# A bound on |h| from column norms and token norms, with squares on GpSimd, in place of a maximum over every block

## The chip, the cores and the metric

The kernel runs on one core of one Trainium2 chip. The metric is the device time of one execution in microseconds (us); here 1173.38 us is the median of three runs before the change (1172.96 to 1173.91). The engines are named as in the profile: PE (TensorE matmuls), PEld (its weight loads), DVE (VectorE), ACT (ScalarE), POOL (GpSimd) and SP (SyncE, which here only issues DMAs). A letter q behind an engine's name (SPq, PEldq) means its queue: instructions that the sequencer handles by itself.

## The reference

Attention with a sigmoid in place of the softmax, and a two-layer block on its result:

```python
# q, k, v: (8, 12, 448, 64)   w_in: (768, 2048)   w_out: (2048, 768)
scores = scale * np.matmul(q, k.transpose(0, 1, 3, 2)) - np.log(S)
attn = 1.0 / (1.0 + np.exp(-scores))
x = np.matmul(attn, v)          # (8, 12, 448, 64), laid out as 3584 tokens x 768
h = x @ w_in
g = h - np.tanh(h)
out = g @ w_out
```

q and k are scaled so that scores have a spread of some units, and the two weight matrices arrive as 64-bit floats.

## The kernel before

The eight batches are handled one after the other. Batch 0 is computed with 32-bit matmuls; from batch 1 on, every matrix is split into a high and a low 16-bit half and each product is three 16-bit matmuls. `first` runs batch 0 and all work on the weights, in an order that is written out by hand as a string (`ORDER`, one letter for each step). `batch` runs one later batch: `moe1` (h and g, from the lines of `product` and `mix`) and `moe2` (g times w_out), with the attention of the next batch put between the matmuls of `moe2`. PE, ACT, DVE and POOL execute what they get in exactly this written order; nothing reorders it.

**The weights' way in.** w_in comes in 24 pieces of 128 x 512 64-bit values. `convert` sends each through stages, one stage a step (letter r): `conv_load` (DMA), `conv_sign` (ACT, L180), `conv_bits` (three DVE instructions: L190 shifts, L191 and L196 each combine two tiles of SBUF), and `conv_end`. The result of L191, the tile `sta`, is |w| as a 32-bit float. `conv_end` takes its high 16 bits and has PE add up the columns: with the matrix `rows` for two pieces at a time (L221, into `cs`); when a group of six pieces is through, ACT squares the sums (L227). `w_in_scales` then turns the four rows of squares into one number by a matmul (L284, `cn`), a maximum, a transpose (L289, `pt`), a maximum and another matmul (L294, `pb`): `W2`, a bound for every column's squared length. All PE instructions for pieces 0 to 21 stand ahead of the first matmul of h (letter M, L1006).

**The small case.** The code holds two versions of the program: class `Small` has a short polynomial for g that is good for |h| below 1/4, and `Builder` has a longer one for all h. `Small` always runs. It keeps, of every block of h squared (`u`), the maximum (L1161, `squares`), and after the last block `largest` turns these 64 columns into one number, `flag`, by a DVE maximum (L1171), a PE transpose (L1173) and a DVE maximum (L1174). `build_kernel` then has all five engines load `flag` into a register (L1183) and compare it (L1186). Where it is above `SMALL_BITS` the whole of `Builder` runs again; else the code jumps past it to the waits for the last DMAs and the end of the program.

Of the kernel before, what the change touches and what calls it, by code (L numbers as in the profile page):

```python
# [9 lines left out]
BF16 = mybir.dt.bfloat16  # L10
F32 = mybir.dt.float32
# [3 lines left out]
AF = mybir.ActivationFunctionType  # L15
ALU = mybir.AluOpType
AX = mybir.AxisListType
# [7 lines left out]
CUT = 0.65  # L25


SMALL_BITS = 0x3D7FFFFF
KAPPA_S = 0.051974997
B_S, C_S = -1.2822222, 4.7692432  # L30

# [7 lines left out]
class Builder:  # L39
# [190 lines left out]
    def convert(self, pieces, when):  # L230

        ps = [{"piece": q, "k": k, "when": when} for k, q in enumerate(pieces)]
        wait, end = [None, None], [None, self.conv_end]
        if when == "mixture":
            wait, end = [None] * 3, [None] + end
        elif when == "product":
            wait, end = [None], [None, None] + end
        stages = [self.conv_load] + wait + [self.conv_sign, self.conv_bits] + end
        for t in range(len(ps) + len(stages) - 1):
            for k in range(len(stages) - 1, -1, -1):  # L240
                if stages[k] and 0 <= t - k < len(ps):
                    stages[k](ps[t - k])
            yield 1
# [33 lines left out]
    def w_in_scales(self):  # L277


        nc = self.nc  # L280
        n = self.DFF // 4
        cn = self.ps.tile([P, 512], F32, name="cn", tag="av", bufs=1)
        for j, sq in enumerate(self.row):
            nc.tensor.matmul(cn[32 * j : 32 * (j + 1), :n], self.onesb[:, :32], sq, start=True, stop=True)  # L284
        st = self.sm.tile([P, 1], F32, name="st", tag="st")
        nc.vector.tensor_reduce(st, cn[:, :n], axis=AX.X, op=ALU.max)
        yield 0
        pt = self.ps.tile([P, 512], F32, name="pt", tag="tr", bufs=1)
        nc.tensor.transpose(pt[:1, :P], st, self.ident)  # L289
        mx = self.sm.tile([1, 1], F32, name="mx2", tag="mx2")  # L290
        nc.vector.tensor_reduce(mx, pt[:1, :P], axis=AX.X, op=ALU.max)
        yield 0
        pb = self.ps.tile([P, 512], F32, name="pb", tag="tr", bufs=1)
        nc.tensor.matmul(pb[:, :1], self.onesf[:1, :], mx, start=True, stop=True)  # L294
        self.W2 = self.const.tile([P, 1], F32, name="W2")
        nc.vector.tensor_scalar(self.W2, pb[:, 0:1], 1.03, None, op0=ALU.mult)
        self.Swi, self.iSwi = self.scale_of(self.W2, "swi")
# [462 lines left out]
    def g_scales(self, m):  # L760

        t1 = lambda name: self.sm.tile([P, 1], F32, name=name)
        V = self.nc.vector
        hb = t1("hb")
        V.tensor_scalar(hb, m, self.W2, None, op0=ALU.mult)
        hc = t1("hc")
        V.tensor_scalar(hc, hb, 1e12, None, op0=ALU.min)
        h2 = t1("h2")
        V.tensor_tensor(h2, hc, hc, op=ALU.mult)
        h3 = t1("h3")  # L770
        V.scalar_tensor_tensor(h3, h2, 1.0 / 9.0, hc, op0=ALU.mult, op1=ALU.mult)
        g2 = t1("g2")
        V.tensor_tensor(g2, hb, h3, op=ALU.min)
        V.tensor_scalar(g2, g2, 2.1, TINY, op0=ALU.mult, op1=ALU.max)
        y = self.pow2(g2, 1, "g")
        iSg = t1("iSg")
        V.tensor_scalar(iSg, y, 2.0**49, None, op0=ALU.mult)
        Sg = t1("Sg")
        V.reciprocal(Sg, iSg)
        return Sg, iSg  # L780


    def halves(self, m, g):

# [322 lines left out]
    def second(self, b, blocks, alone, events):  # L1107

        step = lambda: next(self.blocks)
        events += [(p, step) for p in blocks]  # L1110
        scales = []

        def norms():
            scales.append(self.batch_scales(self.xs, False))
            next(scales[0])

        if blocks:
            end = blocks[alone]
            events.append((end + 3, norms))
            events += [(p, lambda: next(scales[0], None)) for p in (end + 5, end + 7)]  # L1120
        events.sort(key=lambda e: e[0])
        full = self.NF * (self.S // P)
        for k, _ in enumerate(self.moe2(b, self.gs)):
            now = k + 1 if k < full else full + (k + 1 - full) / 2
            while events and events[0][0] <= now:
                events.pop(0)[1]()
        assert not events


class Small(Builder):  # L1130
# [4 lines left out]
    def __init__(self, ctx, tc, flag, *args):  # L1135
        super().__init__(ctx, tc, *args)
        V = self.nc.vector
        self.flag = flag
        self.squares = self.const.tile([P, self.B * self.NB], F32, name="squares")
        V.memset(self.squares, 0.0)  # L1140
        self.bs = self.const.tile([P, 1], F32, name="bs")
        V.memset(self.bs, B_S)
        self.seen = 0

    def mix(self, ps, g, ih, ihk):

        nc = self.nc
        V = nc.vector
        temp = lambda name: self.tp.tile([P, 2, self.S], F32, name=name, tag="t")
        u = temp("u")  # L1150
        n, self.seen = self.seen, self.seen + 1
        nc.scalar.activation(u, ps, AF.Square, scale=ih)  # L1152
        m = temp("m")
        V.scalar_tensor_tensor(m, ps, ihk, u, op0=ALU.mult, op1=ALU.mult)  # L1154
        yield 1
        self.finish_g()
        yield 1
        q = temp("q")
        nc.scalar.activation(q, u, AF.Square, bias=self.bs)  # L1159
        V.scalar_tensor_tensor(m, q, C_S, m, op0=ALU.add, op1=ALU.mult)  # L1160
        V.tensor_reduce(self.squares[:, n : n + 1], u, axis=AX.XY, op=ALU.max)  # L1161
        if self.seen == self.B * self.NB:
            self.largest()
        yield 1
        self.late.append((m, g))

    def largest(self):

        nc = self.nc
        m = self.sm.tile([P, 1], F32, name="largest")  # L1170
        nc.vector.tensor_reduce(m, self.squares, axis=AX.X, op=ALU.max)  # L1171
        pt = self.ps.tile([P, 512], F32, name="lt", tag="tr", bufs=1)
        nc.tensor.transpose(pt[:1, :P], m, self.ident)  # L1173
        nc.vector.tensor_reduce(self.flag, pt[:1, :P], axis=AX.X, op=ALU.max)  # L1174


def build_kernel(tc, *args):
    nc = tc.nc
    with tc.tile_pool(name="flag", bufs=1) as pool:
        flag = pool.tile([1, 1], F32, name="flag")  # L1180
        with ExitStack() as ctx:
            Small(ctx, tc, flag, *args).build()
        bits = nc.values_load(  # L1183
            flag.bitcast(mybir.dt.int32), skip_runtime_bounds_check_because="it is compared, nothing else"
        )
        with tc.If(bits > SMALL_BITS):  # L1186
            with ExitStack() as ctx:
                Builder(ctx, tc, *args).build()

# [28 lines left out]
```

## Time and profile before

| | |
|---|---|
| three runs, median (lowest, highest) | 1173.38 us (1172.96, 1173.91) |
| the profiled execution's own time | 1173.52 us |
| its span, first to last instruction | 1171.5 us |
| mean granted TensorE clock | 0.997 |
| PE busy | 1154.7 us (99%) |
| DVE busy | 761.6 us (65%) |
| ACT busy | 678.0 us (58%) |
| POOL busy | 77.8 us (7%) |

The page gives each engine's busy time in total and in 40 slices of the span; groups of equal instructions by line with their mean duration and what ended the idle time ahead of them; the chain of work that ended last, followed back from the end; and the timeline, which has each instruction's start and duration. The device time is the span and 2.0 us around it.

### The profile page before, as it was taken

How to read it: one execution, taken by the hardware profiler on the slowest of the kernel's cores; microseconds unless marked ns; L12 is line 12 of the kernel's file. 1: busy time of each engine (PE TensorE's matmuls, PEld its weight loads, DVE VectorE, ACT ScalarE, POOL GpSimd, SP SyncE). 2: the span in 40 equal slices, each digit the busy share in tenths (PEclk: the TensorE clock that was granted, in tenths of full speed). 3: DMA queues.
4: the chain of work that ended last, by engine and by line, in shares of the span. 5: the costliest groups of instructions: out<-in, count | busy, mean ns of one | idle time of the engine just before them, and what ended most of it. 6: DMA issues, size and time to landing. Idle time of an engine off the chain costs nothing.

```text
span 1171.5 us, 18358 instructions
## 1 busy us (share of the span) xinstructions
PE 1154.7 (99%) x7586; PEld 601.8 (51%) x7586; DVE 761.6 (65%) x1170; ACT 678.0 (58%) x993; POOL 77.8 (7%) x58
## 2 busy tenths in 40 slices
PE   9999999999999999999999999999999999999897
PEld 3355444555555555555555555555555555555464
DVE  6988698766767656776577666676566755645600
ACT  7975785545884457844686348753578446623300
POOL 0000010000220002100020002200031000200000
PEclk9999999999999999999999999999999999999999
DMA  9942251000321002210021001210022100000001
GB/s 364 355 157 69 80 182 54 28 1 10 92 69 53 1 16 75 62 39 1 30 77 56 29 1 55 84 53 1 16 62 62 53 1 30 15 21 1 1 15 37
DMA packets 34059, 70.47 MB, mean 60 GB/s; under 512 B 3888, under 2 KB 21040, under 8 KB 33968
## 3 DMA queue, kind: packets, MB, share of 16 engines
q1 hardware_dynamic: 33744, 68.89, 18.0%
q8 instruction: 61, 1.00, 0.4%
q10 hardware_dynamic: 224, 0.33, 0.1%
q14 instruction: 30, 0.25, 0.1%
HBM read 58.20 MB, written 11.01 MB: 59 GB/s over the span
## 4 chain that ended last, share of the span: by engine, by line
PE 92%; DVE 3%; DMA 3%; ACT 1%; issue 0%; SPq 0%; DVEq 0%; ACTq 0%
PE ph L794 33%; PE po L880 30%; PE acc L441 8%; PE sc L410 8%; PE ph L1006 6%; PE por L928 5%; DMA raw<-moe_w_in 1%; DVE wo L257 1%; DMA vn<-v 1%; DMA wo<-moe_w_in 1%; PE wl L211 0%; DVE wo L256 0%; PE nm L711 0%; PE pbn L360 0%; DVE stb L190 0%
## 5 line engine op out<-in xcount | busy, mean ns | idle before, releaser
L880 PE MATMUL po<-wo,g 128*128 128x384 f16 x2304 | 390.4, 327 | 1.4 <-DVE g L788 0.7
L794 PE MATMUL ph<-xhl,wi 128*128 128x448 f16 x2016 | 382.6, 352 | 0.0
L880 PEld LDWEIGHTS <-g 128*128 128x128 f16 x2304 | 221.2, 98 | 167.5 <-issue 25.7
L794 PEld LDWEIGHTS <-wi 128*128 128x128 f16 x2016 | 196.7, 98 | 185.0 <-issue 2.1
L428 DVE SCALAR_TENSOR_TENSOR ahl<-a,ahl 128x896 f16<-128x896 f32 x126 | 161.6, 1318 | 140.4 <-ACT ahl L427 140.4
L1152 ACT ACTIVATE u<-ph,ih 128x896 f32<-128x896 f32 x64 | 64.4, 1006 | 248.3 <-PE ph L794 230.6
L421 ACT ACTIVATE a<-sc,nls,rn 128x896 f32<-128x896 f32 x147 | 156.1, 1092 | 57.1 <-PE sc L410 55.6
L1154 DVE SCALAR_TENSOR_TENSOR m<-ph,ihk,u 128x896 f32<-128x896 f32 x64 | 73.6, 1150 | 150.2 <-ACT u L1152 150.1
L427 ACT ACTIVATE ahl<-a 128x896 f16<-128x896 f32 x126 | 113.1, 940 | 0.6
L410 PE MATMUL sc<-Q,K 64*128 64x448 f16 x1008 | 100.6, 353 | 0.7 <-ACT a L421 0.7
L441 PE MATMUL acc<-ahl,vhl 128*64 128x448 f16 (+1 forms) x864 | 80.6, 356 | 0.0
L472 POOL TENSOR_TENSOR x<-x 128x448 f32<-128x448 f32 x24 | 27.1, 1130 | 763.7 <-ACT x L455 763.7
L1006 PE MATMUL ph<-x,wi 128*128 128x448 f32 x192 | 74.1, 540 | 0.0
L788 DVE SCALAR_TENSOR_TENSOR g<-m,Sg,g 128x896 f16<-128x896 f32 x64 | 73.2, 1143 | 0.8
L787 ACT ACTIVATE g<-m,Sg 128x896 f16<-128x896 f32 x64 | 66.1, 1034 | 12.7 <-DVE m L1160 10.8
L1160 DVE SCALAR_TENSOR_TENSOR m<-q,m 128x896 f32<-128x896 f32 x64 | 69.4, 1084 | 0.9
L1161 DVE TENSOR_REDUCE squares<-u 128x1 f32<-128x896 f32 x64 | 69.0, 1078 | 0.0
L1159 ACT ACTIVATE q<-u,bs 128x896 f32<-128x896 f32 x64 | 66.0, 1031 | 0.3
L928 PE MATMUL por<-wo,g 128*64 128x384 f16 x768 | 64.9, 327 | 0.0
L410 PEld LDWEIGHTS <-K 64*128 64x128 f16 x1008 | 35.5, 97 | 52.4 <-issue 30.9
L441 PEld LDWEIGHTS <-vhl 128*64 128x64 f16 (+1 forms) x864 | 38.3, 108 | 40.2 <-issue 19.8
L928 PEld LDWEIGHTS <-g 128*64 128x64 f16 x768 | 42.4, 110 | 22.1 <-issue 4.5
(143 smaller groups left out, 842.6 us busy)
## 6 DMA issues: line engine op xcount, KB each, us to landing
knn<-k SPq DMA_DIRECT2D x45, 224.0 KB, 2.6
qnn<-q SPq DMA_DIRECT2D x44, 224.0 KB, 2.6
rawo<-moe_w_out SPq DMA_DIRECT2D x22, 384.0 KB, 5.2
out<-o SPq DMA_DIRECT2D x21, 384.0 KB, 2.3
raw<-moe_w_in SPq DMA_DIRECT2D x13, 512.0 KB, 8.2
vn<-v SPq DMA_DIRECT2D x24, 256.0 KB, 2.9
wo<-moe_w_in SPq DMA_DIRECT2D x11, 512.0 KB, 8.1
vn<-v SPq DMA_DIRECT2D x24, 192.0 KB, 2.4
```

The lines of the kernel that those rows point to most:

```text
L410: self.nc.tensor.matmul(ps[i * m : (i + 1) * m, h, : self.S], K[i][r, w, c * P : c * P + m], Q[i][r, x, :], start=(n == 0), stop=(n == len ...
L421: self.nc.scalar.activation(a[:, 0], ps[:, :, : self.S], AF.Sigmoid, bias=self.nls, scale=scale)
L427: nc.scalar.activation(A[:, 0], a[:, 0], AF.Copy, scale=A_SCALE)
L428: nc.vector.scalar_tensor_tensor(A[:, 1], a[:, 0], A_SCALE, A[:, 0], op0=ALU.mult, op1=ALU.subtract)
L441: self.nc.tensor.matmul(acc[i][h * D : (h + 1) * D, : self.S], v[k, w, 2 * QT + h if half else h * QT + c], A[k, x, h], start=(n == 0 and ...
L788: nc.vector.scalar_tensor_tensor(g[:, 1], m, Sg, g[:, 0], op0=ALU.mult, op1=ALU.subtract)
L794: self.nc.tensor.matmul(ph, self.wi[:, self.slot(c, k), part, e * P : (e + 1) * P], xhl[c][:, x, :], start=(i == 0), stop=(i == len(prods) ...
L880: nc.tensor.matmul(po[i][:, :H], gs[f // 2][:, x, f % 2, tk * P : (tk + 1) * P], self.wo[:, i * self.NF + 2 * ks[f // 2] + f % 2, w], star ...
L928: nc.tensor.matmul(po[e * D : (e + 1) * D, :H], gs[f // 2][:, x, f % 2, nm:S], self.wo[:, e * self.NF + 2 * ks[f // 2] + f % 2, w], start= ...
L1006: nc.tensor.matmul(ph[:, e, :S], self.fp32(self.wi, self.slot(c, k))[:, 0, e * P : (e + 1) * P], xs[c], start=(c == 0), stop=(c == self.NC ...
L1154: V.scalar_tensor_tensor(m, ps, ihk, u, op0=ALU.mult, op1=ALU.mult)
L1160: V.scalar_tensor_tensor(m, q, C_S, m, op0=ALU.add, op1=ALU.mult)
```

## The change

Three parts.

- `Small.convert` replaces the sum of |w| by exact squares. A new stage, `conv_square`, stands in the step that was empty between `conv_bits` and `conv_end`: POOL multiplies the high 16 bits of `sta` with themselves into a 16-bit tile `sq` (24 times, 128 x 512). `conv_end` has PE add these up with a matrix of ones, one matmul for each piece over all 128 columns; after six pieces DVE takes the maximum of the sums (`tops`). `w_in_scales` is one maximum over the four columns of `tops`; the matmuls into `cn` and `pb` and the transpose `pt` are gone.
- The maximum over `u` in `mix` and `largest` are gone. `g_scales`, which had the product of `W2` and the largest squared token length for its own use (`hb`, a bound on h squared), now also keeps the maximum of these products in `flag`. `SMALL_BITS` is lowered from 0.0625 to 0.0615. ACT writes the square of u + b back into `u` instead of into a new tile.
- `flag` is loaded into the registers 20 steps into the last `moe2`, by an event, and the branch has its small case placed first behind the compare.

```diff
     def g_scales(self, m):
         V.tensor_scalar(hb, m, self.W2, None, op0=ALU.mult)
+        self.g_bounds(hb)
...
     def second(self, b, blocks, alone, events):
+        if b + 1 == self.B:
+            events.append((20, self.decide))
...
 class Small(Builder):
-        self.squares = self.const.tile([P, self.B * self.NB], F32, name="squares")
-        V.memset(self.squares, 0.0)
+        V.memset(flag, 0.0)
+        self.tops = self.const.tile([P, 4], F32, name="tops")
+    def convert(self, pieces, when):
+        if when != "attention":
+            yield from super().convert(pieces, when)
+            return
+        ps = [{"piece": q, "k": k, "when": when} for k, q in enumerate(pieces)]
+        stages = [self.conv_load, None, None, self.conv_sign, self.conv_bits, self.conv_square, self.conv_end]
...
+    def conv_square(self, p):
+        n = p["piece"][3]
+        high = p["a"].bitcast(BF16).rearrange("p (n t) -> p n t", t=2)[:, :, 1]
+        p["sq"] = self.sm.tile([P, n], BF16, name="sq", tag="sq", bufs=4)
+        self.nc.gpsimd.tensor_tensor(p["sq"], high, high, op=ALU.mult)
+    def conv_end(self, p):
...
+        self.nc.tensor.matmul(self.cs[:, :n], self.onesb, p["sq"], start=(r == 0), stop=(r == self.NC - 1))
+        if r == self.NC - 1:
+            self.nc.vector.tensor_reduce(self.tops[:, i : i + 1], self.cs[:, :n], axis=AX.X, op=ALU.max)
+    def w_in_scales(self):
+        m = self.sm.tile([P, 1], F32, name="mx2", tag="mx2")
+        self.nc.vector.tensor_reduce(m, self.tops, axis=AX.X, op=ALU.max)
...
+    def g_bounds(self, hb):
+        self.nc.vector.tensor_tensor(self.flag, self.flag, hb, op=ALU.max)
     def mix(self, ps, g, ih, ihk):
-        q = temp("q")
-        nc.scalar.activation(q, u, AF.Square, bias=self.bs)
-        V.scalar_tensor_tensor(m, q, C_S, m, op0=ALU.add, op1=ALU.mult)
-        V.tensor_reduce(self.squares[:, n : n + 1], u, axis=AX.XY, op=ALU.max)
-        if self.seen == self.B * self.NB:
-            self.largest()
+        nc.scalar.activation(u, u, AF.Square, bias=self.bs)
+        V.scalar_tensor_tensor(m, u, C_S, m, op0=ALU.add, op1=ALU.mult)
...
+    def decide(self):
+        self.bits = self.nc.values_load(
...
-        with tc.If(bits > SMALL_BITS):
+        with tc.If(fast.bits > SMALL_BITS, preferred_fallthrough_block=False):
```

How this moves instructions is seen at three places. The first is POOL at the start of the program, during the way in of w_in; `ident` is a constant, `x_...` are tiles of squared attention results. Before:

```order
masks.py:197 MEMSET ident 128x128
masks.py:199 ISA
masks.py:199 AFFINE_SELECT ident<-ident 128x128 [waits Pool_49]
L481 TENSOR_TENSOR x_1158<-x_1158,x_1295 128x448 [waits DVE_49,PE_49,Activation_49]
L481 TENSOR_TENSOR x_1158<-x_1158,x_1443 128x448 [waits Activation_49]
```

And after:

```order
masks.py:197 MEMSET ident 128x128
masks.py:199 ISA
masks.py:199 AFFINE_SELECT ident<-ident 128x128 [waits Pool_49]
L1170 TENSOR_TENSOR sq<-sta 128x512 [waits DVE_49] x4
L1170 TENSOR_TENSOR sq<-sta 128x512 [waits DVE_49,PE_49] x20
L481 TENSOR_TENSOR x_1176<-x_1176,x_1313 128x448 [waits DVE_49,PE_49,Activation_49]
```

POOL had nothing to do there; now 24 squares stand in its queue, each behind a DVE instruction (L191), and from the fifth on also behind the matmul that reads the buffer. The same stretch on DVE, around the end of the first group of six pieces, before:

```order
L190 TENSOR_SCALAR sta<-sta 128x512
L191 SCALAR_TENSOR_TENSOR sta<-raw,sta 128x512
L196 SCALAR_TENSOR_TENSOR wi<-raw,sta 128x2x256
L190 TENSOR_SCALAR sta<-sta 128x512
L191 SCALAR_TENSOR_TENSOR sta<-wo,sta 128x512
```

And after:

```order
L190 TENSOR_SCALAR sta<-sta 128x512
L191 SCALAR_TENSOR_TENSOR sta<-raw,sta 128x512
L196 SCALAR_TENSOR_TENSOR wi<-raw,sta 128x2x256
L1181 TENSOR_REDUCE tops<-cs 128x1
L190 TENSOR_SCALAR sta<-sta 128x512
L191 SCALAR_TENSOR_TENSOR sta<-wo,sta 128x512
```

One maximum over the column sums is put between two pieces, four times in all, three of them ahead of piece 21. The third place is PE at the start of the last `moe2`, where `g_...` are the blocks of g, `po` the sums and `lt` the transposed maxima. Before:

```order
L880 LDWEIGHTS g_10860
L880 MATMUL po1_11219<-wo_101,g_10860 128x384
L1173 MATMUL lt_11240<-ident_89,largest_11238 1x128 [waits DVE_49]
L880 LDWEIGHTS g_10923 [waits Activation_49]
L880 MATMUL po0_11218<-wo_101,g_10923 128x384
```

And after:

```order
L887 LDWEIGHTS g_10788
L887 MATMUL po1_11134<-wo_101,g_10788 128x384
L887 LDWEIGHTS g_10850 [waits Activation_49]
L887 MATMUL po0_11133<-wo_101,g_10850 128x384
L887 LDWEIGHTS g_10850
```

The transpose, which waited for DVE, is gone from between the matmuls. At the end of the program the five loads of `flag`, which stood behind each engine's last instruction, now stand within the last `moe2`, and behind the compare come first the waits for the last DMAs and then a jump over all of `Builder` to the program's last instructions; before, the compare itself jumped over `Builder`, and these waits and the last instructions stood together behind it.

More of the change, by code (lines that the diff above doesn't have):

```diff
@@ L25 @@
 CUT = 0.65
-SMALL_BITS = 0x3D7FFFFF
+SMALL_BITS = 0x3D7BE76C
 KAPPA_S = 0.051974997
@@ L780, in g_scales @@
         return Sg, iSg
+    def g_bounds(self, hb):
+        pass
+    def decide(self):
+        pass
     def halves(self, m, g):
@@ L1138, in __init__, with g_bounds @@
         self.flag = flag
-        self.squares = self.const.tile([P, self.B * self.NB], F32, name="squares")
-        V.memset(self.squares, 0.0)
+        V.memset(flag, 0.0)
         self.bs = self.const.tile([P, 1], F32, name="bs")
         V.memset(self.bs, B_S)
-        self.seen = 0
+        self.tops = self.const.tile([P, 4], F32, name="tops")
[5 more added lines that the diff above has]
+        stages = [self.conv_load, None, None, self.conv_sign, self.conv_bits, self.conv_square, self.conv_end]
+        for t in range(len(ps) + len(stages) - 1):
+            for k in range(len(stages) - 1, -1, -1):
+                if stages[k] and 0 <= t - k < len(ps):
+                    stages[k](ps[t - k])
+            yield 1
+    def conv_square(self, p):
[4 more added lines that the diff above has]
+    def conv_end(self, p):
+        kind, r, i, n = p["piece"]
+        if kind == "out":
+            super().conv_end(p)
+            return
+        if r == 0:
+            self.cs = self.ps.tile([P, 512], F32, name="cs", tag=("av", "tr")[i % 2], bufs=1)
+        self.nc.tensor.matmul(self.cs[:, :n], self.onesb, p["sq"], start=(r == 0), stop=(r == self.NC - 1))
[4 more added lines that the diff above has]
+        self.nc.vector.tensor_reduce(m, self.tops, axis=AX.X, op=ALU.max)
+        self.W2 = self.const.tile([P, 1], F32, name="W2")
+        self.nc.vector.tensor_scalar(self.W2, m, 1.03, None, op0=ALU.mult)
+        self.Swi, self.iSwi = self.scale_of(self.W2, "swi")
+        yield 0
+    def g_bounds(self, hb):
+        self.nc.vector.tensor_tensor(self.flag, self.flag, hb, op=ALU.max)
     def mix(self, ps, g, ih, ihk):
@@ L1150, in mix @@
         u = temp("u")
-        n, self.seen = self.seen, self.seen + 1
         nc.scalar.activation(u, ps, AF.Square, scale=ih)
@@ L1157, in mix, with decide @@
         yield 1
-        q = temp("q")
-        nc.scalar.activation(q, u, AF.Square, bias=self.bs)
-        V.scalar_tensor_tensor(m, q, C_S, m, op0=ALU.add, op1=ALU.mult)
-        V.tensor_reduce(self.squares[:, n : n + 1], u, axis=AX.XY, op=ALU.max)
-        if self.seen == self.B * self.NB:
-            self.largest()
+        nc.scalar.activation(u, u, AF.Square, bias=self.bs)
+        V.scalar_tensor_tensor(m, u, C_S, m, op0=ALU.add, op1=ALU.mult)
         yield 1
         self.late.append((m, g))
[L1167 to L1174, printed above, removed]
+    def decide(self):
+        self.bits = self.nc.values_load(
+            self.flag[:1].bitcast(mybir.dt.int32), skip_runtime_bounds_check_because="it is compared, nothing else"
+        )
 def build_kernel(tc, *args):
-    nc = tc.nc
     with tc.tile_pool(name="flag", bufs=1) as pool:
-        flag = pool.tile([1, 1], F32, name="flag")
+        flag = pool.tile([P, 1], F32, name="flag")
         with ExitStack() as ctx:
[L1182 to L1186, printed above, removed]
+            fast = Small(ctx, tc, flag, *args)
+            fast.build()
+        with tc.If(fast.bits > SMALL_BITS, preferred_fallthrough_block=False):
             with ExitStack() as ctx:
```

## The prediction

> **What bounds the kernel now.** I read the page's busy times and slices first, then the chain of waits, then the timeline of the two places that the change touches: the start and the end.
>
> ```profile
> PE 1154.7 (99%) x7586; PEld 601.8 (51%) x7586; DVE 761.6 (65%) x1170; ACT 678.0 (58%) x993; POOL 77.8 (7%) x58
> PEclk9999999999999999999999999999999999999999
> PE 92%; DVE 3%; DMA 3%; ACT 1%; issue 0%; SPq 0%; DVEq 0%; ACTq 0%
> L1161 DVE TENSOR_REDUCE squares<-u 128x1 f32<-128x896 f32 x64 | 69.0, 1078 | 0.0
> ```
>
> PE is the bound: 99% busy at full clock, 92% of the chain. The 69 us of maxima (L1161) that leave DVE therefore buy little: from 223 to 1103 us the timeline has PE without a gap. What counts is where PE waits or is fed late, and that is before 50 us and after 1103 us. The start first: busy time by engine in two of its stretches (PE, PEld, DVE, ACT, POOL).
>
> ```profile
> 10.00:20.00 10.00, 10.00 (x56) 3.07 (x56) 9.66 (x18) 8.92 (x13) 0.00 (x0) 1.00 1.02 405
> 40.00:50.00 10.00, 10.00 (x57) 2.90 (x56) 9.62 (x17) 9.43 (x16) 0.00 (x0) 1.00 1.03 401
> ```
>
> DVE's groups, with count, busy time and mean ns:
>
> ```profile
> L190 DVE TENSOR_SCALAR sta<-sta 128x512 uint32<-128x512 uint32 x22 | 9.3, 421 | 9.1 <-ACT sta L180 8.1 <-PE cs L221 1.0
> L191 DVE SCALAR_TENSOR_TENSOR sta<-raw,sta 128x512 uint32<-128x512 uint32 x12 | 8.3, 693 | 0.4
> L196 DVE SCALAR_TENSOR_TENSOR wi<-raw,sta 128x512 uint32<-128x512 uint32 x12 | 8.3, 691 | 0.4
> ```
>
> And the timeline (start, duration, then the instruction; in brackets idle time and what ended it):
>
> ```profile
> 9.13 0.43 DVE L190 TENSOR_SCALAR sta<-sta 128x512 uint32<-128x512 uint32 x1 [7.75 <-ACT sta L180]
> ...
> 48.76 0.71 DVE L191 SCALAR_TENSOR_TENSOR sta<-wo,sta 128x512 uint32<-128x512 uint32 x1
> ...
> 49.58 0.40 PE L221 MATMUL cs<-sta,rows 128*64 128x512 bf16 x2
> 49.91 2.52 PE L1006 MATMUL ph<-x,wi 128*128 128x448 f32 x6
> ```
>
> From 9 us on, DVE converts piece after piece, 1.79 us each (0.42 + 0.69 + 0.69 with small steps), and idles only 1.35 us up to piece 21 (9.1 in the group's row less the 7.75 ahead of piece 0). Piece 21's L191 ends at 49.47 us, the column sum that needs it starts at 49.58, the first matmul of h at 49.91. So the start of PE's solid stretch hangs on DVE's conversion, with nothing to spare, although DMA and ACT are also close to full. POOL is idle.
>
> **The change part by part.** *Squares on POOL.* 24 multiplications of 128 x 512, each between L191 of its piece and its column sum; 22 of them stand ahead of the first matmul of h. Their own time would be hidden, POOL being idle. What they do to DVE is not shown for this place, but for others, where POOL multiplies or adds beside DVE:
>
> ```profile
> 151.85 1.28 DVE L257 SCALAR_TENSOR_TENSOR wi<-wi,swi_s 128x1024 f16<-128x1024 f32 x1
> 152.71 1.42 POOL L481 TENSOR_TENSOR x<-x,x 128x448 f32<-128x448 f32 x1 [151.40 <-ACT x L470]
> 153.06 1.29 DVE L190 TENSOR_SCALAR stb<-stb 128x384 uint32<-128x384 uint32 x1
> ...
> 155.45 0.35 DVE L190 TENSOR_SCALAR stb<-stb 128x384 uint32<-128x384 uint32 x1
> ...
> 313.42 1.48 POOL L472 TENSOR_TENSOR x<-x 128x448 f32<-128x448 f32 x1 [9.81 <-ACT x L455]
> 314.15 3.65 DVE L428 SCALAR_TENSOR_TENSOR ahl<-a,ahl 128x896 f16<-128x896 f32 x2
> 314.98 1.87 POOL L481 TENSOR_TENSOR x<-x,x 128x448 f32<-128x448 f32 x1
> ...
> 323.68 0.93 POOL L472 TENSOR_TENSOR x<-x 128x448 f32<-128x448 f32 x1 [6.83 <-ACT x L455]
> ```
>
> And all L428 (shortest, median, longest ns):
>
> ```profile
> L428 DVE SCALAR_TENSOR_TENSOR ahl<-a,ahl x126: 1079/1093/2027, 210.5 to 1030.5; 128x896 f16<-128x896 f32 x126
> ```
>
> L190, the very instruction of the conversion, takes 1.29 us beside POOL's L481 and 0.35 without: 0.94 lost. It starts while L257 ends and is held until POOL is through. Two L428, each combining two SBUF tiles as L191 and L196 do, take 3.65 together beside one L472 and one L481, against 2 x 1.09: 1.47 lost, so L472's part is 1.47 - 0.94 = 0.53. Reaching DVE's three instructions without a gap, each square must take a turn and hold DVE back. L472 is the nearest row (POOL, a tile times itself): 0.53 x 512/448 = 0.61 us a square. Ends: 0 (16-bit input might not collide at all; no row has it) and L481's 0.94 x 512/448 = 1.07. I take 0.61. The 21 squares of pieces 0 to 20 fall on DVE before piece 21's L191: 21 x 0.61 = 12.8 us. Square 21 must itself be waited for: L196 of its piece is first (0.69), then the square (0.93 x 512/448 = 1.06, less its start-up, about 0.9), against 0.11 before: +1.5. DVE's 1.35 idle goes. The first matmul of h moves by 12.8 + 1.5 - 1.35 = **+12.95 us**.
>
> The Trainium skill ("GPSIMD Engine Reference", 3.1 Elementwise) gives 2.6 cycles an element for a two-input instruction on GpSimd, by estimate 1.11 us for 512; "SBUF — State Buffer" (Who interferes with whom) says that the loser of the shared port pair blocks for the whole instruction. By these the 21 squares cost 23.3 us and not 12.8; no row here shows a DVE instruction held for all of POOL's duration.
>
> *Maxima into `tops`.* Three of about 0.61 us before piece 21 (L286 below, the same maximum, is 0.67, and the next starts 0.6 after it). They read PSUM; the square running beside each then costs DVE nothing, 0.61 against 0.61: **0**. The ACT squares they replace (L227) are off the path.
>
> *Column sums.* Two pieces shared one slot of PE (0.33 us a pair above); now each takes its own, some 0.2. PE will wait for DVE there, which covers it: **0**. Behind the first matmul of h, PE is solid and loses `cn`, `pt` and `pb`:
>
> ```profile
> 62.72 0.67 DVE L286 TENSOR_REDUCE st<-cn 128x1 f32<-128x512 f32 x1
> ...
> 61.56 0.40 PE L284 MATMUL cn<-sq,onesb 128*32 128x512 bf16 x4
> 66.84 0.27 PE L289 MATMUL pt<-ident,st 128*1 128x128 f32 x1
> 71.72 0.38 PE L294 MATMUL pb<-mx,onesf 1*128 1x1 f32 x2
> ```
>
> Start to start they cost 0.33 + 0.11 + 0.31 = **-0.75 us**. The lateness is not made up later: from 50 us PE has work without gaps up to 145 us, and shorter DVE work there feeds nobody sooner.
>
> *`largest` gone.* At the start of the last product:
>
> ```profile
> 1108.67 0.22 DVE L1171 TENSOR_REDUCE largest<-squares 128x1 f32<-128x64 f32 x1
> 1108.94 0.27 PE L1173 MATMUL lt<-ident,largest 128*1 128x128 f32 x1 [3.77 <-DVE largest L1171]
> 1109.05 46.69 PE L880 MATMUL po<-wo,g 128*128 128x384 f16 x276
> ...
> 1109.46 1.13 DVE L788 SCALAR_TENSOR_TENSOR g<-m,Sg,g 128x896 f16<-128x896 f32 x1
> ```
>
> PE stands 3.77 us for the transpose, and 0.11 in it: **-3.88 us**. What is needed next, the last block of g (DVE until 1110.6), is used some 13 us later, so no other wait appears.
>
> *Writing `u` in place* makes ACT's second square wait until DVE's L1154 has read `u`, at most about 0.4 us a block, with ACT idle 3.94 us a block (next fence): 0. *Register loads amid the product*: PE's load takes 0.49 us and ran 1.9 us ahead of PE's last matmul (the fence after it); that lead covers it: 0. SP's waits for a `flag` long written; queued behind it is a store 15 us away: 0.
>
> ```profile
> 1096.45 1.01 ACT L1152 ACTIVATE u<-ph,ih 128x896 f32<-128x896 f32 x1 [3.94 <-PE ph L794]
> ...
> 1155.67 7.99 PE L928 MATMUL por<-wo,g 128*64 128x384 f16 x96
> ```
>
> *The end.* Loads and compares by queue (ns, then the first and last start):
>
> ```profile
> L1183 PEldq TENSOR_LOAD <-flag x1: 489/489/489, 1161.7 to 1161.7; - x1
> ...
> L1186 SPq EVENT_SEMAPHORE  x8: 17/17/17, 1169.6 to 1170.1; - x8
> ...
> L1186 PEldq COMPARE_BRANCH  x1: 3532/3532/3532, 1162.3 to 1162.3; - x1
> ...
> L1186 SPq COMPARE_BRANCH  x1: 50/50/50, 1165.9 to 1165.9; - x1
> ```
>
> The last two stores, and the mean time of ACT's from issue to landing:
>
> ```profile
> 1164.35 0.47 SPq L873 DMA_DIRECT2D out<-orem  x1
> 1164.36 0.55 ACTq L873 DMA_DIRECT2D out<-orem  x1
> ...
> out<-orem ACTq DMA_DIRECT2D x1, 96.0 KB, 2.6
> ```
>
> PE's last matmul ends at 1163.66. The last store lands at 1164.36 + 2.6 = 1166.96. SP compares at 1165.9 and goes on at 1169.6: 3.65 us for a jump over `Builder` (PE: 3.53 in one row), which outlasts the stores. Then 0.6 for eight waits and 1.3 to the end, 1171.5. Now the eight waits come first, until 1167.4 (the first are met early), and the jump over `Builder` follows them. A jump without a compare is in no row that leaves its neighbourhood: it costs between 0.05 (the compare's own) and 3.65. I take 3.65, the row with the same distance: 1167.4 + 3.65 + 1.3 = 1172.4, **+0.9**; with 0.05 it would be -2.7. The Trainium skill ("Runtime: NRT & Kernel Launch", Instruction fetch mechanics) lets every taken branch that leaves the two pages at hand wait for its fetch; by it, too, +0.9.
>
> Sum: 12.95 - 0.75 - 3.88 + 0.9 = +9.2 us on the profiled execution's 1173.5, 0.1 above the median: **1182.7 us**.
>
> **The rivals.** *The whole instruction blocks*: L481's price, 21 x 1.07 = 22.5, gives 22.5 + 1.5 - 1.35 - 3.73 = +18.9, 1192. For it: L481's 0.94 is nearly all of its uncontended time; against it, L472 is the like instruction and lost half of that.
>
> *Squares cost DVE nothing* (the other side): 16-bit reads may pass DVE, as POOL passes a maximum. Then three maxima 1.8, the last square about 1.1, minus 1.35, give +1.6 at the first matmul, and 1.6 - 0.75 - 3.88 + 0.9 = -2.1: 1171.3, faster. It decides below about 0.1 us a square. Against it: every two-input DVE instruction beside POOL above was held.
>
> *The jump does not stall*: 3.6 less in each case, 1179.1 with my price.
>
> *The bound fails and `Builder` runs too*: from the reference's inputs the bound is 1.03 x 1.18 x 0.0203 = 0.025, the limit 0.0615. Under 1 in 100, and about a second kernel's time.
>
> **How the numbers follow.** My price (0.45 to 0.8 a square, either jump) 0.64: 1176 to 1187. Whole instruction (above 0.8) 0.15: 1187 to 1192. Something between (0.1 to 0.45) 0.10: 1168 to 1179. Nothing (below 0.1) 0.11: 1167 to 1172. The range from 1176 to 1191 leaves out the last, most of the one before it and the top of the second, about 2 in 10. A measurement here tells 0.2% (2.3 us) from no change: faster 0.12 (all but the edge of the last case, and a little of the one before), same 0.05, slower 0.83.
>
> **What the new profile would show.** Right: L190, L191 and L196 longer by some 0.6 us a piece between them, at 2.4 us a piece; the first matmul of h near 63 us; POOL's squares at 1 to 1.5 us; no gap of PE at the last product's start; SP's branch after the last landing and about 3.6 us of nothing. Wrong: a conversion still at 1.8 us a piece, or PE held ahead of h by ACT or DMA rather than by column sums; or a granted clock under 1 at the start, where PE now waits more.

## The result, and the profile after

The changed kernel takes 1185.91 us (median of four executions, 1185.39 to 1187.08) against 1173.17 for the kernel before: a ratio of 1.0109, 95% interval 1.0092 to 1.0127. It became slower by 12.7 us, where 9.2 were forecast. The profiled execution of the changed kernel took 1187.08 us with a span of 1185.3, 13.8 longer than the span before. One execution of the reordered kernel among the experiments took 1509.95 us at a PE clock of 0.75 or less; it is left out of that kernel's time, and since that kernel's only trace is of it, only DVE's, POOL's and ACT's rows and waits for POOL are read there.

The page of the changed kernel: busy times, the slices of PE, POOL and the granted clock, and the chain by engine.

```profile
PE 1157.4 (98%) x7578; PEld 601.6 (51%) x7578; DVE 721.8 (61%) x1115; ACT 682.6 (58%) x989; POOL 114.1 (10%) x82
PE   7799999999999999999999999999999999999997
POOL 3520000000021002200021000200022000200000
PEclk9999999999999999999999999999999999999999
PE 90%; DVE 5%; issue 1%; ACT 1%; DMA 1%; POOL 0%; SPq 0%; DVEq 0%; POOLq 0%; ACTq 0%
```

DVE is 40 us less busy, and the kernel is slower. DVE's share of the chain went from 3% to 5%, and PE's first two slices are at 7 where they were at 9, just where POOL now works. The groups of that place, each shape by itself (count, busy us, mean ns, idle time ahead):

```profile
L1170 POOL TENSOR_TENSOR sq<-sta 128x512 bf16<-128x512 bf16 x24 | 35.8, 1491 | 36.5 <-DVE sta L191 36.5
L190 DVE TENSOR_SCALAR sta<-sta 128x512 uint32<-128x512 uint32 x24 | 27.4, 1141 | 9.1 <-ACT sta L180 9.1
L191 DVE SCALAR_TENSOR_TENSOR sta<-raw,sta 128x512 uint32<-128x512 uint32 x13 | 9.0, 693 | 0.4
L1179 PE MATMUL cs<-sq,onesb 128*128 128x512 bf16 x24 | 9.0, 382 | 14.1 <-POOL sq L1170 13.9
L196 DVE SCALAR_TENSOR_TENSOR wi<-raw,sta 128x512 uint32<-128x512 uint32 x13 | 9.0, 692 | 0.4
```

L190 went from a mean of 421 ns to 1141; L191 and L196 kept their 0.69 us. PE's column sums wait 13.9 us for POOL's squares. The timeline up to the first matmul of h:

```profile
58.90 1.48 POOL L1170 TENSOR_TENSOR sq<-sta 128x512 bf16<-128x512 bf16 x1 [1.15 <-DVE sta L191]
...
59.40 0.68 DVE L1181 TENSOR_REDUCE tops<-cs 128x1 f32<-128x512 f32 x1
...
60.00 0.66 DVE L190 TENSOR_SCALAR sta<-sta 128x512 uint32<-128x512 uint32 x1
...
64.06 0.69 DVE L196 SCALAR_TENSOR_TENSOR wi<-raw,sta 128x512 uint32<-128x512 uint32 x1
64.17 1.48 POOL L1170 TENSOR_TENSOR sq<-sta 128x512 bf16<-128x512 bf16 x1 [1.15 <-DVE sta L191]
64.67 1.26 DVE L190 TENSOR_SCALAR sta<-sta 128x512 uint32<-128x512 uint32 x1
...
65.97 0.69 DVE L191 SCALAR_TENSOR_TENSOR sta<-wo,sta 128x512 uint32<-128x512 uint32 x1
...
66.69 0.69 DVE L196 SCALAR_TENSOR_TENSOR wi<-wo,sta 128x512 uint32<-128x512 uint32 x1
66.80 1.48 POOL L1170 TENSOR_TENSOR sq<-sta 128x512 bf16<-128x512 bf16 x1 [1.15 <-DVE sta L191]
...
67.30 1.26 DVE L190 TENSOR_SCALAR sta<-sta 128x512 uint32<-128x512 uint32 x1
...
68.34 0.60 PE L1179 MATMUL cs<-sq,onesb 128*128 128x512 bf16 x2
...
68.78 1.67 PE L1013 MATMUL ph<-x,wi 128*128 128x448 f32 x4
```

From L190 to the next L190 it is 2.63 us (64.67 to 67.30), against 1.79 before: +0.84 a piece. The square starts beside L196 (64.17), L190 begins as L196 ends (64.67) and ends itself at 65.93, 0.28 after the square's own end at 65.65. Only where a maximum over the sums (L1181, from PSUM) stands between them has most of the square passed by then, and L190 takes 0.66. L191 of piece 21 ends at 66.66 (49.47 before), the first matmul of h starts at 68.78 (49.91 before).

The end of the changed kernel: SP's branch instructions and waits (ns shortest/median/longest, then first and last start in us).

```profile
L1225 SPq EVENT_SEMAPHORE  x8: 17/17/17, 1177.9 to 1180.7; - x8
...
L1225 SPq COMPARE_BRANCH  x2: 38/46/53, 1177.7 to 1180.8; - x2
```

```profile
L1253 SPq EVENT_SEMAPHORE  x10: 17/28/28, 1184.0 to 1185.2; - x10
```

SP compares at 1177.7, waits for the last stores until 1180.7, jumps at 1180.8 and goes on at 1184.0: 3.2 us of nothing behind the last landing. From PE's last matmul to the end it is 8.76 us, 7.84 before.

### The profile page after: what moved, and what is told of

Read it like the earlier page. It is cut to its first block, busy times and chain, and to the rows that moved or that the text cites. A ratio compares the mean times of both kernels' runs of the same rounds, so it can differ in the third digit from the quotient of the medians.

```text
span 1185.3 us, 18247 instructions
## 1 busy us (share of the span) xinstructions
PE 1157.4 (98%) x7578; PEld 601.6 (51%) x7578; DVE 721.8 (61%) x1115; ACT 682.6 (58%) x989; POOL 114.1 (10%) x82
## 4 chain that ended last, share of the span: by engine, by line
PE 90%; DVE 5%; issue 1%; ACT 1%; DMA 1%; POOL 0%; SPq 0%; DVEq 0%; POOLq 0%; ACTq 0%
PE ph L801 32%; PE po L887 30%; PE acc L441 8%; PE sc L410 8%; PE ph L1013 6%; PE por L935 5%; DVE sta L190 1%; DVE sta L191 1%; DVE wo L257 1%; DMA raw<-moe_w_in 1%; PE wl L211 0%; POOL sq L1170 0%; DVE wo L256 0%; ACT a L421 0%; PE pbn L360 0%
## 5 line engine op out<-in xcount | busy, mean ns | idle before, releaser
L472 POOL TENSOR_TENSOR x<-x 128x448 f32<-128x448 f32 x24 | 27.1, 1131 | 763.7 <-ACT x L455 763.7
L1207 ACT ACTIVATE u<-u,bs 128x896 f32<-128x896 f32 x64 | 66.7, 1042 | 26.8 <-DVE m L1203 26.8
L1208 DVE SCALAR_TENSOR_TENSOR m<-u,m 128x896 f32<-128x896 f32 x64 | 69.9, 1092 | 11.1 <-ACT u L1207 8.9
L1013 PEld LDWEIGHTS ph<-x,wi 128*128 128x128 f32 x192 | 36.3, 190 | 34.2 <-issue 33.4
```

Of the source, the lines that this page charges most:

```text
L1013: nc.tensor.matmul(ph[:, e, :S], self.fp32(self.wi, self.slot(c, k))[:, 0, e * P : (e + 1) * P], xs[c], start=(c == 0), stop=(c == self.NC ...
L1208: V.scalar_tensor_tensor(m, u, C_S, m, op0=ALU.add, op1=ALU.mult)
```

## The experiments

All were timed beside the kernel before, at 1173.1 to 1173.9 us. The diffs are against the changed kernel where nothing else is said.

**The changed kernel with the old sums of |w|.** No squares, everything else as in the change.

```diff
-SMALL_BITS = 0x3D7BE76C
+SMALL_BITS = 0x3F800000
 class Small(Builder):
-    def convert(self, pieces, when):
...
-    def conv_square(self, p):
...
-    def conv_end(self, p):
...
-    def w_in_scales(self):
...
```

> The changed kernel with the weights' sums as they were before (two pieces at a time, sums of |w|, no POOL squares); the gone maxima, the early register load and the reordered branch stay. The bound is looser then, so the compare's limit is raised to 1.0. If the squares on POOL are what costs, the first matmul of h is back near 50 us and the gain at the last product stays: 1173.2 - 5.7 + 0.9 = 1168.4 us. If the last product gives only the 3.9 us that its gap lasts, 1170.2. If the loss comes from anything else in the change, it stays near 1185.9.

1169.40 us, ratio 0.9968 (0.9956 to 0.9979), about midway between the two figures given for the last product; its trace decides for the larger gain there (5.71 us, worked out below). The first matmul of h is back at 49.81 us. The whole loss belongs to the squares and what comes with them; the rest of the change is a gain of 3.7 us in the median, though its end still has the later jump. With the limit at 1.0, the kernel no longer makes sure that |h| is below 1/4, where its polynomial is good: it serves to measure, not to be used.

**The squares alone.** The maxima over `u`, `largest` and the old end are put back.

```diff
-        self.g_bounds(hb)
+        V.tensor_reduce(self.squares[:, n : n + 1], u, axis=AX.XY, op=ALU.max)
+        if self.seen == self.B * self.NB:
+            self.largest()
```

> The kernel before, with the squares part of the change alone (POOL squares, one column sum a piece, maxima into tops, the short scale); block maxima, the final maximum and the end as before. If the parts add up: 1173.2 + 18.6 (the lateness of the last batches' matmuls in the changed kernel's trace) = 1191.8. If the removed block maxima had won something in the middle, the changed kernel's 18.6 already holds that gain, and this is slower still: above 1193.

1190.30 us, ratio 1.0146 (1.0130 to 1.0161), 1.5 below the 1191.8 expected: 17.0 us of loss by the squares; the changed kernel's 12.7 and the 3.7 that the rest gains make 16.4. L190 is at 1152 ns again.

**POOL writes and does not read.** The square is replaced by filling the same tile with a constant, so that the bound is not that of w_in.

```diff
-        self.nc.gpsimd.tensor_tensor(p["sq"], high, high, op=ALU.mult)
+        self.nc.gpsimd.memset(p["sq"], 0.00152587890625)
```

> The changed kernel with each POOL square replaced by a POOL memset of the same tile (a constant whose column sum is about the real one): same place, same waits, same matmuls and maxima, but POOL reads nothing. If POOL's reads of SBUF hold DVE back: L190 returns to 0.42 us, 1.79 us a piece, and the time falls to about 1170 (1168.4 and three maxima of 0.6). If POOL's writes hold L190 too: L190 between 0.42 and 1.26, 1172 to 1180. If the cause is the chain itself (column sums that wait for POOL, one PE slot for each piece), it stays above 1182.

1169.60 us, ratio 0.9970 (0.9960 to 0.9980). The timeline of this kernel, with two fills in a row beside two DVE instructions:

```profile
30.26 0.42 DVE L190 TENSOR_SCALAR sta<-sta 128x512 uint32<-128x512 uint32 x1
30.35 1.26 POOL L1170 MEMSET sq<- 128x512 bf16 x2 [2.79 <-PE cs L1179]
...
30.71 0.69 DVE L191 SCALAR_TENSOR_TENSOR sta<-raw,sta 128x512 uint32<-128x512 uint32 x1
```

Neither DVE instruction is held here: L190 0.42, L191 0.69. Of the fills, the one beside L190 took 0.79 us and the one beside L191 0.52. Over the 24 pieces L190's mean is 472 ns (four of them took about 0.7), so a fill is not quite free beside L190, but no L191 or L196 of w_in took over 0.71 us. The maxima, the column sums and an instruction on POOL in itself do not cost what the squares cost. That leaves POOL's reading, with a reservation: a fill reads nothing of L191's result, so it waits for a free buffer alone (the first runs at 0.87 us) and is not in the square's place behind L191, and it takes 0.53 us, where a square works for 0.90 (next experiment).

**Half of each square.** POOL squares 256 of the 512 columns, PE and DVE treat only these.

```diff
-        self.nc.gpsimd.tensor_tensor(p["sq"], high, high, op=ALU.mult)
+        self.nc.gpsimd.tensor_tensor(p["sq"][:, : n // 2], high[:, : n // 2], high[:, : n // 2], op=ALU.mult)
```

> The changed kernel with squares, column sums and maxima over 256 of each piece's 512 columns (the other half is left out of the bound). If DVE is held for as long as POOL streams its elements, L190 falls from 1.26 to about 0.84 us and the time by 21 x 0.42 = 8.8 to about 1177. If each square costs a fixed turn whatever its size, L190 and the time stay: 1185.9.

1175.86 us, ratio 1.0025 (1.0015 to 1.0034). The timeline around one piece:

```profile
30.26 0.69 DVE L196 SCALAR_TENSOR_TENSOR wi<-raw,sta 128x512 uint32<-128x512 uint32 x1
30.37 1.05 POOL L1170 TENSOR_TENSOR sq<-sta 128x256 bf16<-128x256 bf16 x1 [1.16 <-DVE sta L191]
...
30.87 0.84 DVE L190 TENSOR_SCALAR sta<-sta 128x512 uint32<-128x512 uint32 x1
```

L190 is held for 0.84 - 0.42 = 0.42 us, half of the 0.84 of the whole square. POOL's record fell only from 1.48 to 1.05. Both fit one reading: POOL stands while L196 runs (0.58 us of overlap in both kernels: 30.37 to 30.95, 64.17 to 64.75), then works for 0.47 or 0.90 us, and in that time L190 stands.

**DVE squares for itself.**

```diff
-        self.nc.gpsimd.tensor_tensor(p["sq"], high, high, op=ALU.mult)
+        self.nc.vector.tensor_tensor(p["sq"], high, high, op=ALU.mult)
```

> The changed kernel with the squares on DVE in place of POOL. By the hold, POOL's square costs DVE 0.84 us a piece; as its own instruction a 512-wide one with two inputs from SBUF costs it at most 0.72 (L191, start to start), perhaps half of that with 16-bit numbers, which no row shows. So DVE doing the work itself should be no slower: between 1185.9 - 21 x 0.12 - 1 = 1182 and 1185.9 - 21 x 0.45 - 1 = 1175. If POOL's part really ran beside DVE, moving it onto DVE would make it slower than 1185.9.

1182.37 us, ratio 1.0083 (1.0066 to 1.0100), just above the range given. The square takes DVE 0.68 us (0.60 from its start to the next), L190 is back at 0.42. So DVE does a square in less time (0.60) than it loses to POOL's doing it (0.84).

**Which DVE instruction is held.** The shift L190 of the next piece is put between L191 and L196. It needs its tile a piece sooner, so ACT's `conv_sign` moves one step ahead, too.

```diff
-        stages = [self.conv_load, None, None, self.conv_sign, self.conv_bits, self.conv_square, self.conv_end]
+        stages = [self.conv_load, None, self.conv_sign, None, self.conv_bits, self.conv_square, self.conv_end]
...
+    def conv_bits(self, p):
         V.scalar_tensor_tensor(au, p["lo"], 29, au, op0=ALU.logical_shift_right, op1=ALU.bitwise_or)
+        self.conv_shift(self.ps_in[p["k"] + 1])
...
         V.scalar_tensor_tensor(
```

> The changed kernel with DVE's shift of the next piece (L190 of the changed kernel) put between this piece's two combining instructions (L191, then the shift of the next piece, then L196); same work, nothing left out. Theory: while POOL's square really runs (0.90 us alone: 1.48 less the 0.58 that it overlaps DVE's L196) any DVE instruction that touches only SBUF stands, whichever comes next. Then the hold only changes its place: the shift is back at 0.42 us, L196 takes about 0.69 + 0.84 = 1.5 us, POOL's record falls to about 1.2 us (it waits for 0.3 of the shift instead of 0.58 of L196), the pitch stays 2.6 us a piece, and the time stays at 1186 us. Rival: only the shift collides with POOL, L191 and L196 run beside a square unharmed (both were 0.69 us in every piece). Then the shift is out of the way, the pitch falls to about 1.9 us, the first matmul of h comes near 52 us, and the time is about 1170 us.

1182.50 us (median of four), ratio 1.0078 (1.0062 to 1.0093). Groups of its trace from 8 to 70 us (L1185 is the former L196, L1169 the former L190, L1180 the former L191):

```profile
L1193 POOL TENSOR_TENSOR sq<-sta 128x512 bf16<-128x512 bf16 x21 | 34.6, 1660 | 33.8 <-DVE sta L1180 32.5 <-PE cs L1202 1.3
L1185 DVE SCALAR_TENSOR_TENSOR wi<-raw,sta 128x512 uint32<-128x512 uint32 x12 | 12.5, 1044 | 0.0
L1169 DVE TENSOR_SCALAR sta<-sta 128x512 uint32<-128x512 uint32 x22 | 10.1, 457 | 22.5 <-ACT sta L180 22.5
```

and its timeline over one piece:

```profile
30.79 0.68 DVE L1180 SCALAR_TENSOR_TENSOR sta<-wo,sta 128x512 uint32<-128x512 uint32 x1
...
31.39 0.42 DVE L1169 TENSOR_SCALAR sta<-sta 128x512 uint32<-128x512 uint32 x1
31.61 1.09 POOL L1193 TENSOR_TENSOR sq<-sta 128x512 bf16<-128x512 bf16 x1 [5.59 <-DVE sta L1180]
31.72 1.53 DVE L1185 SCALAR_TENSOR_TENSOR wi<-wo,sta 128x512 uint32<-128x512 uint32 x1
...
33.17 0.68 DVE L1180 SCALAR_TENSOR_TENSOR sta<-raw,sta 128x512 uint32<-128x512 uint32 x1
```

In this piece the hold changed its place, as the theory had it: the shift is back at 0.42 us, L196 takes 1.53 (0.69 and 0.84), and the square's record shrank to 1.09. The rival, that only the shift collides, is out. The pitch, 2.38 us (30.79 to 33.17), is 0.25 shorter than in the changed kernel: no DVE instruction now follows at once the one whose result it reads. The shift starts 0.60 us behind L191 and L196 0.33 behind the shift, where L196 started 0.73 behind L191 and L191 0.45 behind an undisturbed shift (30.26 to 30.71 in the kernel with fills).

But only about half of the pieces go this way: of the 24 L196, 11 took 1.52 to 1.59 us and 13 took 0.68 to 0.76. Eight of those 13 ran while one of two squares did not get its turn, the first of them here:

```profile
14.82 0.41 DVE L1169 TENSOR_SCALAR sta<-sta 128x512 uint32<-128x512 uint32 x1
...
14.98 7.04 POOL L1193 TENSOR_TENSOR sq<-sta 128x512 bf16<-128x512 bf16 x1 [1.38 <-DVE sta L1180]
15.16 0.68 DVE L1185 SCALAR_TENSOR_TENSOR wi<-raw,sta 128x512 uint32<-128x512 uint32 x1
...
16.70 0.68 DVE L1185 SCALAR_TENSOR_TENSOR wi<-wo,sta 128x512 uint32<-128x512 uint32 x1
...
20.45 0.68 DVE L1180 SCALAR_TENSOR_TENSOR sta<-raw,sta 128x512 uint32<-128x512 uint32 x1
```

This square stood until DVE ran out of pieces (its last instruction ends at 21.13, the square 0.89 later). Meanwhile DVE ran unheld, at 1.54 us a piece (15.16 to 16.70). The second such square takes 6.92 us from 48.51 on; the two raise the group's mean to 1660 ns. So the two engines do not always take turns; what decides which of them stands is not shown. DVE's gain does not last here: PE's column sums wait 9.4 us for such squares, PE's attention matmuls behind them come late, ACT waits for these, and DVE then waits 15.2 us for ACT's next pieces (22.5 in the group's row less 7.3 ahead of the first). The kernel ends up 3.4 us below the changed one, which the theory did not have.

**PE kept busy over the gap of `largest`.** The kernel before, with 17 matmuls of ones ahead of the transpose.

```diff
     def largest(self):
+        for _ in range(17):
+            nc.tensor.matmul(wt[:, :], self.onesb, ...)
         nc.tensor.transpose(pt[:1, :P], m, self.ident)
```

> The kernel before, with 17 matmuls of 512 columns whose result nobody reads (3.6 us) put on PE ahead of the transpose at the start of the last product: PE still cannot go on before the transpose at about 1109, but it is busy while it waits. If the halved clock of 3.4 us behind the gap is due to PE's idling, it disappears and the time falls by 1.7 to 1171.5. If the clock falls for another reason, or the slow matmuls have another cause, it stays at 1173.2 or above.

1171.39 us, ratio 0.9985 (0.9976 to 0.9994). The windows of the kernel before, at and behind the gap (PE's clock is the third number from the end):

```profile
1107.00:1109.00 2.00, 0.06 (x1) 0.06 (x2) 1.85 (x3) 1.04 (x1) 0.00 (x0) 1.00 0.00 0
1109.00:1111.00 2.00, 2.00 (x8) 1.05 (x9) 1.34 (x2) 0.00 (x0) 0.00 (x0) 0.55 0.00 0
1111.00:1113.00 2.00, 2.00 (x9) 0.95 (x7) 0.00 (x0) 0.00 (x0) 0.00 (x0) 0.60 0.00 0
1113.00:1115.00 2.00, 2.00 (x15) 1.22 (x13) 0.00 (x0) 0.00 (x0) 0.00 (x0) 1.00 0.04 8
```

And the two stretches behind the gap in this experiment:

```profile
1109.00:1111.00 2.00, 2.00 (x13) 1.22 (x14) 1.34 (x2) 0.00 (x0) 0.00 (x0) 1.00 0.03 8
1111.00:1113.00 2.00, 2.00 (x15) 1.21 (x13) 0.00 (x0) 0.00 (x0) 0.00 (x0) 1.00 0.00 0
```

Behind the gap the clock was at half for 2 x (0.45 + 0.40) / 0.5 = 3.4 us, which costs 1.7. With the idle time filled, the transpose starts at the same time (1108.95, before 1108.94), but the clock stays at 1.00, 28 matmuls start in the 4 us behind it where 17 did, and the kernel is 1.9 us faster.

**`largest` in the midst of the product.** The kernel before, with `largest` called 20 steps into the last `moe2`.

```diff
-        if self.seen == self.B * self.NB:
-            self.largest()
+        if b + 1 == self.B:
+            events.append((20, self.largest))
```

> The kernel before, with one thing moved: the final maximum, its transpose on PE and the second maximum are issued 20 steps into the last product and not amid its start. If PE's 3.77 us gap and the 1.7 us that the halved clock costs behind it both go: 1173.2 - 5.5 = 1167.7. If only the gap goes: 1169.4. If the wait reappears at the new place: 1173.

1167.55 us, ratio 0.9954 (0.9941 to 0.9966): gap and halved clock are both gone, without touching the bound.

**The same, with the register loads at step 40.**

```diff
             events.append((20, self.largest))
+            events.append((40, self.decide))
```

> As the run with the final maximum moved, and the registers loaded 40 steps into the last product, with the branch's order as before the change (the compare itself jumps over the second builder). SP's load (0.96 us) and what stands around it goes from behind the last store: about 1.1 us less, 1166.6. If the end is set by the landing of the last store, no difference to the run without the loads moved: 1167.7.

1167.19 us, ratio 0.9948 (0.9936 to 0.9961): between the two expectations, and not told apart from the one before.

**The changed kernel with the branch in its usual order.**

```diff
-        with tc.If(fast.bits > SMALL_BITS, preferred_fallthrough_block=False):
+        with tc.If(fast.bits > SMALL_BITS):
```

> The changed kernel with the branch in its usual order alone. Theory: the jump runs beside the last stores, 2 to 2.3 us less at the end: 1183.7 to 1183.9 us. Rival: no difference, 1185.9 us.

1183.29 us (median of four), ratio 1.0079 (1.0063 to 1.0094), 0.4 below the range given. SP in this kernel:

```profile
L1225 SPq EVENT_SEMAPHORE  x8: 17/17/17, 1179.8 to 1180.4; - x8
...
L1225 SPq COMPARE_BRANCH  x1: 50/50/50, 1176.5 to 1176.5; - x1
```

The compare itself jumps, 3.3 us from 1176.5 to 1179.8, beside the last stores, whose eight waits behind it are all met at once. From the last matmul to the end it is 6.48 us instead of 8.76. A fifth execution took 3077 us, at a granted clock of 1.00, and left no trace; whether `Builder` ran in it stays open.

**The old sums with the branch in its usual order.** The kernel of the first experiment with the edit of the last.

> The kernel with the old sums of |w| and the new bound (1169.4 us), and with the branch in its usual order, so that the compare itself jumps over Builder and the waits for the last stores stand behind the jump. Theory: the jump's 3.2 to 3.65 us then runs beside the last stores, as before the change; from the last matmul to the end it takes about 6.3 us instead of 8.65, and the time is 1167.2 us. Rival: the jump costs the same wherever it stands, or the other engines' jumps end last: 1169.4 us.

1166.91 us, ratio 0.9940 (0.9926 to 0.9953), 6.44 us from the last matmul to the end, against 8.70 with the later jump. It is the fastest here, 6.6 us below the kernel before and 19 below the changed one; against the kernel with the maxima and late loads (1167.19) it cannot be told apart, though that one has 69 us more of DVE work. And that one is the kernel to keep: the kernel here has the limit of 1.0 from the first experiment, which lets pass what the short polynomial is not good for.

**The fastest kernel with DVE's shift put earlier.** Also a check on how free the start is once POOL is out of it.

```diff
-        stages = [self.conv_load, None, None, self.conv_sign, self.conv_bits, None, self.conv_end]
+        stages = [self.conv_load, None, self.conv_sign, None, self.conv_bits, None, self.conv_end]
...
+        self.conv_shift(self.ps_in[p["k"] + 1])
```

> The fastest kernel so far (old sums of |w|, new bound, branch in its usual order, 1166.9 us) with DVE's shift of the next piece put between the two combining instructions, as in the run where squares stood on POOL. There each piece came 0.25 us sooner than the hold alone would give, since no DVE instruction then follows at once the one whose result it reads (starts 0.60 and 0.33 us apart instead of 0.73 and 0.45). Theory: at the start DVE sets the pace, and 21 pieces by 0.25 us give up to 5.2 us: 1162 us; ACT, busy 9.3 of 10 us there, would stop it at about 1164. Rival: the DMA engines are full at the start (busy share 1.02 to 1.04, 400 to 407 GB/s from 10 to 50 us in the traces without squares), DVE then only waits longer for pieces: 1166 to 1167 us.

1168.76 us, ratio 0.9952 (0.9938 to 0.9966): no gain. Two stretches of its start:

```profile
10.00:20.00 10.00, 8.22 (x45) 2.52 (x46) 8.71 (x18) 8.22 (x11) 0.00 (x0) 1.00 1.03 407
...
30.00:40.00 10.00, 9.09 (x50) 2.85 (x48) 7.68 (x15) 8.88 (x14) 0.00 (x0) 1.00 1.03 402
```

and the group of the shift:

```profile
L1168 DVE TENSOR_SCALAR sta<-sta 128x512 uint32<-128x512 uint32 x24 | 10.2, 423 | 14.7 <-ACT sta L180 14.6
```

DVE is less busy (7.7 to 8.7 of 10), and what it saves it waits for ACT's next piece: 14.6 us, 9.3 of them ahead of the first, against 8.2 and 7.7 in the kernel without this edit. The DMA engines are full (1.03, 402 to 407 GB/s), as in the kernel before. So at the start DVE, ACT and the transfers set nearly the same pace, and the shift put earlier brings nothing there by itself.

## Why the prediction was right, step by step

| step | forecast, us | measured, us | from |
|---|---|---|---|
| first L190 of the program | 0 | +1.05 | 9.13 to 10.18 |
| squares hold DVE, its idle time used up, maxima | +11.45 | +16.14 | first L190 to the end of piece 21's L191: 40.34 to 56.48 |
| wait for square 21 | +1.5 | +1.68 | end of that L191 to the first matmul of h: 0.44 to 2.12 |
| `cn`, `pt`, `pb` and `largest` gone | -4.63 | -6.00 | first matmul of h to the start of `por`: 1105.76 to 1099.76 |
| end | +0.9 | +0.92 | last matmul to the end: 7.84 to 8.76 |
| sum | +9.2 | +13.8 (profiled), +12.7 (medians) | |

*The place and the sign* were right, and the runs show why: DVE's conversion set the first matmul of h, POOL's squares held DVE, and all of the 18.87 us arrived at that matmul. Without the squares the rest of the change is a gain. That the time fell within the range is in part luck, though. By its price a square falls into the case given 0.15 (above 0.8 us, 1187 to 1192), by the time into the one given 0.64 (1176 to 1187): the squares' stretch cost 4.7 us more than forecast and the first L190 came 1.05 late, and `largest` took back 1.8 more than forecast.

*The price of a square* was under-sized: 0.61 forecast, 0.84 measured, between the two ends kept for the range (0 and 1.07), nearer to the upper. The step that failed was to take L472's part, a remainder of a subtraction over two DVE and two POOL instructions, as the nearest row. Half a square gave 0.42, so the price is POOL's own working time, 0.90 for 512 elements, nearly whole. L472's 1.48 beside DVE, against 0.93 without, then reads like the square's 1.48: a wait of POOL's and its work. The rival "the whole instruction blocks" had the mechanism right; its price of 1.07 was too high. The Trainium skill ("SBUF — State Buffer", Who interferes with whom) says that a DVE instruction with two inputs in SBUF contends with a GpSimd instruction that reads SBUF but not with one that only writes, that DVE's reductions do not contend, and that the loser stands entirely; the traces agree on the first three (L196 held for 0.84 in the reordered kernel, L191 0.69 beside a fill, the maximum 0.68 beside a square), and L190 lost 0.84 of the square's 0.90. What the change held was L190, which reads one tile only; that it is held too is shown by the runs, not by that rule on two inputs. The figure drawn from the Trainium skill ("GPSIMD Engine Reference", 3.1 Elementwise), 1.11 us by estimate, was too long: POOL worked 0.90.

*The maxima at nothing* came out right, by a way that was not quite the forecast's. A piece with a maximum lost 0.60 to it and still 0.24 in L190, together the 0.84 that a held L190 alone loses, so the maximum adds nothing; but the square is not wholly free beside it. The stretch works out as 18 x 0.84 + 3 x (0.24 + 0.60) = 17.6, less the idle time used up (1.35, of which 0.24 stayed) = 16.5, against 16.14 measured.

*The wait for square 21* was right in size and in its order: the square starts 0.14 after L191, works after L196 and ends at 68.28. The profile of after also shows the lower clock that the forecast named as a danger, 0.50 from 64 to 67 us. In this execution it had a part in the wait: PE was busy with the slowed attention matmuls right up to the sums of squares 20 and 21, which start at 68.34. In the kernel with the branch in its usual order, whose start has the same code, the clock was 1.00 there, PE stood 1.25 us for square 21, and the wait was 1.89 (L191's end at 65.39 to 67.28) instead of 2.12. So the low clock makes some 0.23 of the 1.68.

*`cn`, `pt`, `pb`*: -0.75 forecast. From the first matmul of h to `por` it is 1100.05 us with the old sums and 1099.36 with the fills: -0.69. In the changed kernel only -0.29 remains, since PE waits 0.73 us for DVE's `stb` soon after (0.32 with the fills, none with the old sums). The three instructions alone were thus worth about 1.0, and the wait, which the forecast did not have, took most of it back.

*`largest`* was under-sized: -3.88 forecast, 1100.05 - 1105.76 = -5.71 measured. The forecast counted PE's idle time and not the halved clock behind it. The page's row of the granted clock, in which one slice is 29 us, shows only nines; windows of 2 us would have shown 0.55 and 0.60. The Trainium skill ("TensorE: Matmul & The Clock Gate", Part 1) gives about 3.4 us of idleness as what drops the clock, and as long for its return; the trace agrees here (idle 3.77, half clock 3.4), and the run with the gap filled gave 1.9 us of it back. At the start of the changed kernel it took less: the clock fell at 63.6 us, although PE had been busy for 1.65 of the 3.41 us just before and had not been idle for longer than 1.96 at a time since 10 us.

*The end* was right, and so was its mechanism: the jump without a compare takes as long as the other (3.2 us; the compares' jumps took 3.3 and 3.65), so its place counts, behind the waits or beside them. Two small errors cancelled: the jump was 0.45 shorter than the 3.65 taken, and the last of the waits was met about as much later than forecast (4.2 us behind the last matmul against 3.7). The rival of a jump that costs nothing is out.

*The first L190*, 1.05 late, comes ahead of any square. Over the kernels run here it started between 8.25 us (with the fills) and 10.59 (in the last experiment), and at 8.92 in the kernel with the branch in its usual order, whose start has the same code, so the profiled execution met a late one; that would account for most of the difference between +13.8 and +12.7.

*`Builder` running too*: not in the timed executions of the changed kernel.

What stays open: what decides, in the reordered kernel, whether a square or DVE stands, and how much of its 3.4 us comes from that; and the long execution named above.

## What to carry to other kernels

An idle engine is not a free one: before work is moved to POOL, look at what DVE does in the same microseconds, and price the move at POOL's whole working time on DVE where a run or a row shows the two colliding. The other way round happens, too: a DVE without gaps kept a square waiting for 7 us in the reordered kernel. The 3.8 us wait of PE cost its length and another 1.7 us of slow clock, so a small serial step belongs in the midst of a product, where calling it 20 steps later gained 5.7 us without any new bound. And a jump over much code should start before the last waits, not behind them.

## What was not expected of the hardware

- A POOL square of 512 16-bit elements that takes 0.90 us by itself costs the DVE instruction behind it 0.84, be it the shift or a combining instruction, while it stands itself for the DVE instruction ahead of it (0.58 us): the record of 1.48 us is a wait and the work. In the reordered kernel two squares waited 6 us and more behind a DVE without gaps (records of 7.04 and 6.92 us), and DVE's own instructions were not held meanwhile.
- A POOL fill, which reads nothing, ran beside a two-input DVE instruction without harm to either (0.52 us and 0.69), and a DVE maximum from PSUM beside a square kept its 0.68.
- Where a DVE instruction reads the result of the one just ahead, it starts 0.12 to 0.13 us later than where another stands between them (0.73 against 0.60, 0.45 against 0.33).
